# Attention with beacon keys and a maxout feed-forward layer: batch 0 loaded as FP32 by the hardware queue, and a new order of the first two batches

## Chip, cores and metric

One core of one Trainium2 chip (trn2). The metric is the device time of one execution in microseconds (us), the median of several runs; lower is better.

A core has TensorE (PE, with PEld for its weight loads), VectorE (DVE), ScalarE (ACT), GpSimd (POOL) and SyncE (SP), each with its own queue of instructions taken in order. Transfers are asked for by SP, ACT or POOL and carried out by 16 DMA engines. A transfer asked for by POOL (software queue) can change FP32 to BF16 on its way; one asked for by SP or ACT (hardware queue) can't.

## The reference

```python
B, H, S, Nb, D = 8, 8, 576, 16, 64
k_all = concatenate([beacon_k, k], axis=2)            # 592 keys
v_all = concatenate([beacon_v, v], axis=2)
scores = q @ k_all^T / sqrt(D)
scores = where(causal, -1e9, scores)                  # beacons are seen by every query
a = exp(scores - max); a /= a.sum(-1) + 1e-9
x = (a @ v_all).transpose(0, 2, 1, 3).reshape(4608, 512)
h = maximum(maximum(x @ w1, x @ w2), x @ w3)          # 512 -> 768
out = h @ w_out                                       # 768 -> 512, FP32
```

## The kernel before, in words

**Units.** Heads are taken in pairs (32 pairs, `p`), two pairs are a quad (16 quads), two quads a batch. For a pair, queries and keys stand transposed in `qT` and `kT` (128 rows: two heads of 64). `emit_scores` makes scores with keys along the partitions, in four groups for each pair (`groups`), and ACT takes their exponential into `at` (L532). `emit_masks` zeroes what lies above the diagonal, on POOL or on DVE (L549, L551). `emit_pv` multiplies by values and by ones (the sums) for a quad and a half of the tokens (288), four heads side by side in 32 columns of the array each (L592); `invert_sums` and `multiply` (L624) divide into `xT`.

**Feed-forward.** Blocks of 512 tokens; a block has 22 units. For block 0 these are nine `mm1_halves` for the first 256 tokens (kind 0), nine for the others (kind 1), and four `mm2_unit` with `w_out` (kind 2). Other blocks have 18 `mm1_unit` (L654) and four `mm2_unit` (L690). A kind 0 unit needs the first half of batch 0 in `xT`, kind 1 the second half too. `hT` collects the maximum over the three weight matrices on DVE.

**Order.** Each engine's order is the order in which the program is written. Batches 0 and 1, with units laid between them, are written out in `first_steps`; from quad 4 on (batch 2) a loop in `emit_all` follows a table of units, `gaps`, and what is left of the feed-forward ends the kernel. The change touches `first_steps` and what it calls, not the loop.

**Batch 0's queries and keys.** A half (288 tokens) of a pair is 96 rows of 2 heads x 3 tokens x 64. The first halves of pairs 0 and 1 come as FP32 by hardware queues (`load_half`) and are cast by ACT or DVE (`cast_half`, L220); the other three half quads come as BF16 by POOL's software queue (`load_quad`, L229). `turn_half` (L431) transposes with the identity: the two heads do not lie side by side, so each 96x128 transpose is two of 64 columns (L443), to two column places of the array. Batch 1 comes whole by the software queue (`load_whole_quad`), later pairs by SP with a cast on POOL.

**Fillers.** `spare` (L481) multiplies a tile of ones into a bank that is about to be overwritten; `fill` (L411) transposes it. `("scores", p, gi, n)` puts n spares ahead of the scores, `("half", p, h, bank, engine, n, m)` n fills ahead of the keys' transposes and m ahead of the queries'.

**Third key tile of batch 0.** For the first half of the tokens only 48 rows of tile 2 are needed, and `rows_of` (L99) takes just these in L592 and in the masks; the keys behind them are set to zero (L151).

**Gates.** A load with "dve" or "pool" as its last argument has that engine write one element of the destination first, and so waits for that engine's queue.

## Time and profile before

| | us |
|---|---|
| median of 3 runs | 293.68 (293.66 to 293.98) |
| the profiled execution's own time | 294.65 |
| its span, first to last instruction | 292.6 |

| stretch (us) | PE busy | DVE | ACT | POOL | GB/s |
|---|---|---|---|---|---|
| 30 to 40 | 9.91 of 10 | 7.19 | 5.95 | 2.80 | 212 |
| 40 to 50 | 9.32 | 6.85 | 6.38 | 4.52 | 158 |
| 50 to 60 | 9.58 | 7.85 | 8.88 | 5.98 | 222 |
| 60 to 70 | 8.66 | 4.95 | 3.25 | 2.70 | 223 |
| 200 to 250 | 49.52 of 50 | 30.29 | 23.41 | 14.77 | 80 |
| 250 to 292.6 | 39.02 of 42.6 | 20.20 | 5.49 | 0.00 | 50 |

PE's busy time holds fillers, which do no work that is used. GB/s counts bytes as written: a software transfer with cast reads twice as much. The steps of `first_steps` fill PE's first 58 us or so. Over the whole span PE is busy 96%, DVE 58%, ACT 51%, POOL 40%.

### The profile page before, as it was taken

What the parts mean: (1) busy time and instruction counts of PE and PEld (TensorE: products, weight loads), DVE (VectorE), ACT (ScalarE), POOL (GpSimd) and SP (SyncE); (2) the same over time, 40 slices, a digit from 0 to 9 for tenths busy, and PEclk for the clock granted to TensorE, in tenths of its full rate; (3) what the DMA queues carried; (4) which work ended last, traced back from release to release, by engine and by line L of the source; (5) the groups of instructions that cost most, each with busy time, mean ns of one, the idle gap of its engine ahead of it and who ended that gap; (6) DMA issues with size and microseconds to landing.
All of it is one profiled execution on the core that took longest, in us unless ns stands there. A gap on an engine that the chain in (4) does not pass through costs nothing.

```text
span 292.6 us, 8864 instructions
## 1 busy us (share of the span) xinstructions
PE 281.3 (96%) x3714; PEld 160.1 (55%) x3739; DVE 169.6 (58%) x319; ACT 150.5 (51%) x242; POOL 115.8 (40%) x238
## 2 busy tenths in 40 slices
PE   8889999989999999999999999999999999999995
PEld 4656677754454555454545887545454545444442
DVE  1555567837756575566655656565656564474273
ACT  3786576853566676846676256635663552200300
POOL 3618415742546583426454655466323420000000
PEclk9999999999999999999999999999999999999999
DMA  7999979999989999998999899999442003001103
GB/s 131 161 175 185 217 123 225 228 192 261 229 230 256 232 281 270 186 175 263 314 190 181 233 256 268 177 205 214 104 68 98 2 0 137 11 0 74 71 1 143
DMA packets 85111, 49.50 MB, mean 169 GB/s; under 512 B 64208, under 2 KB 79824, under 8 KB 85072
## 3 DMA queue, kind: packets, MB, share of 16 engines
q1 hardware_dynamic: 78864, 43.40, 66.6%
q0 software_dynamic: 5648, 5.21, 11.7%
q8 instruction: 29, 0.48, 0.7%
q10 hardware_dynamic: 560, 0.33, 0.4%
q14 instruction: 10, 0.08, 0.1%
HBM read 35.13 MB, written 14.22 MB: 169 GB/s over the span
## 4 chain that ended last, share of the span: by engine, by line
PE 86%; DMA 7%; POOL 2%; ACT 2%; DVE 1%; issue 1%; POOLq 0%
PE pv L654 21%; PE sc L654 15%; PE wide L654 8%; PE pv L690 6%; PE sc L690 6%; PE sc L517 5%; PE pv L592 4%; DMA w_out_sb<-in_moe_w_out_dram 4%; PE wide L690 3%; PE wide L592 3%; PE sc L592 3%; PE wide L517 3%; DMA w_sb<-in_moe_w_dram 3%; PE pv L481 2%; PE pv L673 1%
## 5 line engine op out<-in xcount | busy, mean ns | idle before, releaser
L532 ACT ACTIVATE at_sb<-sc 128x736 bf16<-128x736 f32 (+5 forms) x91 | 76.5, 867 | 59.3 <-PE sc L517 59.1
L551 POOL TENSOR_SCALAR_AFFINE_SELECT at_sb<-at_sb 128x256 bf16<-128x256 bf16 (+3 forms) x140 | 51.9, 387 | 117.3 <-ACT at_sb L532 117.1
L654 PEld LDWEIGHTS <-w_sb 128*128 128x128 bf16 x648 | 61.1, 98 | 60.4 <-issue 4.7
L654 PE MATMUL pv<-xT,w_sb 128*128 128x512 bf16 (+1 forms) x315 | 65.3, 347 | 0.3
L654 PE MATMUL sc<-xT,w_sb 128*128 128x512 bf16 (+1 forms) x205 | 45.6, 363 | 0.7 <-issue 0.2
L532 ACT ACTIVATE at_sb<-wide 128x736 bf16<-128x736 f32 (+3 forms) x37 | 31.3, 846 | 22.4 <-PE wide L517 22.4
L664 DVE TENSOR_TENSOR hT<-hT,pv 128x512 bf16<-128x512 bf16 x48 | 32.4, 686 | 13.0 <-PE pv L654 13.0
L690 PEld LDWEIGHTS <-hT 128*128 128x128 bf16 x210 | 19.6, 98 | 24.3 <-issue 1.1
L248 POOL CAST p<-st 96x768 bf16<-96x768 f32 x40 | 32.0, 824 | 0.0
L624 DVE TENSOR_TENSOR xT<-pv,recip 128x288 bf16<-128x288 f32 (+2 forms) x48 | 14.2, 350 | 26.7 <-ACT recip L614 26.7
L517 PE MATMUL sc<-qT,kT 64*128 64x288 bf16 (+6 forms) x290 | 27.2, 275 | 2.0 <-POOL at_sb L551 0.6
L664 DVE TENSOR_TENSOR hT<-hT,sc 128x1024 bf16<-128x1024 bf16 (+1 forms) x18 | 19.6, 1098 | 12.7 <-PE sc L654 12.5
L517 PEld LDWEIGHTS <-kT 64*128 64x128 bf16 x400 | 14.9, 94 | 21.8 <-issue 14.7
L592 PEld LDWEIGHTS <-v_sb 128*32 128x32 bf16 (+1 forms) x1408 | 24.7, 96 | 2.6 <-issue 1.3
L654 PE MATMUL wide<-xT,w_sb 128*128 128x512 bf16 (+1 forms) x110 | 24.5, 364 | 0.1
L690 PE MATMUL sc<-w_out_sb,hT 128*128 128x512 bf16 x79 | 19.1, 380 | 1.0 <-DMA w_out_sb<-in_moe_w_out_dram 0.7
L690 PE MATMUL pv<-w_out_sb,hT 128*128 128x512 bf16 x83 | 19.9, 380 | 0.1
L304 POOL CAST v_sb<-st 128x1536 bf16<-128x1536 f32 (+2 forms) x21 | 18.4, 895 | 0.0
L662 DVE CAST hT<-pv 128x512 bf16<-128x512 f32 x20 | 13.7, 688 | 4.8 <-PE pv L654 4.8
L673 PEld LDWEIGHTS <-w_sb 128*128 128x128 bf16 x144 | 13.1, 98 | 3.9 <-issue 1.4
L614 ACT ACTIVATE recip<-lnd 128x288 f32<-128x288 f32 x32 | 14.2, 444 | 1.0
L592 PEld LDWEIGHTS <-ones 128*32 128x32 bf16 (+2 forms) x512 | 11.0, 95 | 6.7 <-issue 4.7
(116 smaller groups left out, 286.3 us busy)
## 6 DMA issues: line engine op xcount, KB each, us to landing
st<-in_q_dram SPq DMA_DIRECT2D x24, 288.0 KB, 5.3
st<-in_k_dram SPq DMA_DIRECT2D x24, 288.0 KB, 5.7
st<-in_v_dram SPq DMA_DIRECT2D x24, 256.0 KB, 5.8
out_dram<-y SPq DMA_DIRECT2D x9, 512.0 KB, 3.3
out_dram<-y SPq DMA_DIRECT2D x17, 256.0 KB, 2.7
w_sb<-in_moe_w_dram POOLq DMA_DIRECT2D x6, 384.0 KB, 7.2
q_dram<-p SPq DMA_DIRECT2D x16, 144.0 KB, 3.1
k_dram<-p SPq DMA_DIRECT2D x16, 144.0 KB, 3.2
```

Of the source, the lines that this page charges most:

```text
L248: cast(t16.rearrange("p r h d -> p h r d"), st[0:QP, i * NQ2 : (i + 1) * NQ2].rearrange("p (h r d) -> p h r d", h=2, r=QR),)
L304: cast(v_sb[0:n, t:t1].rearrange("p t h d -> p (t h d)"), st[0:n, (t - t_lo) * H * D : (t1 - t_lo) * H * D],)
L517: nc.tensor.matmul(ps[:, e, off : off + q1 - q0], kT[hs, 128 * t : 128 * t + 128], qT[hs, q0:q1], start=True, stop=True, tile_position=(64 ...
L532: nc.scalar.activation(out=both_heads(p, gi), in_=ps[:, :, 0 : g_width(p, gi)], func=AF.Exp, scale=scale)
L551: nc.gpsimd.affine_select(out=view, in_=view, compare_op=ALU.is_ge, fill=0.0, base=x0, pattern=[[0, 2], [1, hi - lo]], channel_multiplier=-1,)
L592: nc.tensor.matmul(ps[bank][32 * j : 32 * j + 32, lo + q0 - qa : lo + qb - qa], lhsT, at_view(PPQ * quad + j // 2, t, j % 2, q0, qb), star ...
L614: nc.scalar.activation(out=recip, in_=lnd, func=AF.Exp, scale=-1.0)
L624: nc.vector.tensor_mul(xT[:, 2 * g + part - 1, c0 + ca : c0 + cb], ps[bank][:, lo : lo + cb - ca], recip[:, ca:cb],)
L654: nc.tensor.matmul(dst[:, o0 : o0 + n], w_in[i][:, ct, 128 * (ft + f) : 128 * (ft + f + 1)], xT[:, ct, x0 : x0 + n], start=(ct == 0), stop ...
L664: nc.vector.tensor_max(h, h, ps)
L673: nc.tensor.matmul(ps[:, f], w_in[i][:, ct, 128 * (ft + f) : 128 * (ft + f + 1)], xT[:, ct, tb * TOKB + lo : tb * TOKB + hi], start=(ct == 0),
L690: nc.tensor.matmul(ps[:, t - tt] if two else ps, hT[:, ft, 128 * t : 128 * (t + 1)], w_out_sb[:, ft, :], start=(ft == 0), stop=(ft == n_ft ...
```

## The change

Batch 0's queries and keys all come as FP32 by hardware queues: `load_half` for the first halves of pairs 0 and 1, and the new `load_half_quad` (two pairs in one transfer, into the stage tiles) for the rest. Each half of a pair is cast by an engine named in the step (16 casts for four), and the cast lays the two heads side by side, so that `turn_column` transposes 128 columns at once; batch 1's transposes stay in two. Fills become full transposes there, and spares have 512 columns, not 320. `rows_of` goes: all of the tile's 128 rows are used. The beacons' tiles have 128 rows, the rest zero, and are turned by a plain matmul with the identity. For block 0 the third weight matrix is taken in six units of 512 tokens (kind 3) in place of three units each of kinds 0 and 1, which now have six each. Values may have three banks ("ring+", `passes_3`), without the cut of the last part at `CUT`. `first_steps` is a new list, with other engines for many copies, casts and masks, other fillers and other gates.

```diff
-    K2 = Nb + HALF - 256
-
-    def rows_of(p, t, q1):
-        return K2 if p < PPB and t == 2 and q1 <= HALF else k_rows[t]
...
-    half_pool = ctx.enter_context(tc.tile_pool(name="half", bufs=2))
+    half_pool = ctx.enter_context(tc.tile_pool(name="half", bufs=3))
...
-    bk16_0 = const.tile([Nb, H, D], BF16, name="bk16_0")
+    bk16_0 = const.tile([128, H, D], BF16, name="bk16_0")
+    nc.vector.memset(bk16_0, 0.0)
     bk32_1 = const.tile([NB_PE - Nb, H, D], FP32, name="bk32_1")
-    bk16_1 = const.tile([NB_PE - Nb, H, D], BF16, name="bk16_1")
+    bk16_1 = const.tile([128, H, D], BF16, name="bk16_1")
+    nc.vector.memset(bk16_1, 0.0)
     bk32 = const.tile([NB_DMA, H, D], FP32, name="bk32")
...
-    busy = const.tile([128, 320], BF16, name="busy")
+    busy = const.tile([128, 512], BF16, name="busy")
...
+        stage["half", p, 0, i] = st
+
+    def load_half_quad(g, h, i, queue):
+        key = ("half quad", g, h)
+        st = stage[key] if key in stage else new_stage(key)
+        if i == 1:
+            stage.pop(key)
+        st = st[0:QP, i * NQ2 : i * NQ2 + 4 * HR * D].rearrange("p (h r d) -> p h r d", h=4, r=HR)
+        queue.dma_start(
+            out=st.rearrange("p h r d -> p h (r d)"), in_=half_source(g, h, i, 0, 4)
         )
-        stage["half16", p, 0, i] = t16
+        for j in range(PPQ):
+            stage["half", PPQ * g + j, h, i] = st[:, 2 * j : 2 * j + 2]
+
+    def cast_half(p, i, cast, h=0):
+        t16 = half_pool.tile([QP, HR, 2, D], BF16, name=f"h16{i}")
+        cast(t16.rearrange("p r h d -> p h r d"), stage.pop(("half", p, h, i)))
+        stage["half16", p, h, i] = t16
...
-        ps = sc_psum.tile([128, PPB, n], BF16, name="sc")
+        ps = sc_psum.tile([128, PPB, n], FP32, name="sc")
         for pi in range(PPB):
-            nc.tensor.transpose(
+            nc.tensor.matmul(
                 ps[:, pi],
                 src[:, 2 * pi : 2 * pi + 2].rearrange("p h d -> p (h d)"),
-                ident[0:n, 0:n],
+                ident[:, 0:n],
+                start=True,
+                stop=True,
             )
...
+    def turn_column(dst, src, n):
+
+        if len(src.shape) == 2 and src.shape[1] == 128:
+            nc.tensor.transpose(dst, src, ident[0:n, 0:n])
+            return
+        for e in range(2):
+            nc.tensor.transpose(
+                dst[64 * e : 64 * e + 64],
+                src[:, e],
+                ident[0:n, 0:n],
+                tile_position=(0, 64 * e),
+            )
+
+    def fill(ps, n, wide):
+        src = busy[0:QP, 0:128]
         for i in range(n):
             x0 = 512 + QP * (i % 5)
-            for e in range(2):
-                nc.tensor.transpose(
-                    ps[64 * e : 64 * e + 64, x0 : x0 + QP],
-                    busy[0:QP, 0:64],
-                    ident[0:QP, 0:QP],
-                    tile_position=(0, 64 * e),
-                )
+            turn_column(
+                ps[:, x0 : x0 + QP], src if wide else src.rearrange("p (e d) -> p e d", e=2), QP
+            )
...
-            fill(bank, idle if i == 1 else idle_q)
+            wide = src.shape[1] == HR
+            fill(bank, idle if i == 1 else idle_q, wide)
             for r in range(HR):
-                for e in range(2):
-                    nc.tensor.transpose(
-                        ps[64 * e : 64 * e + 64, r * QP : (r + 1) * QP],
-                        src[:, e, r],
-                        ident[0:QP, 0:QP],
-                        tile_position=(0, 64 * e),
-                    )
+                x = src[:, r].rearrange("p h d -> p (h d)") if wide else src[:, :, r]
+                turn_column(ps[:, r * QP : (r + 1) * QP], x, QP)
             x0 = i * Nb + HALF * h
...
-    def spare(ps, n, cols=320):
+    def spare(ps, n, cols=512):
...
-                    return at[p][0 : rows_of(p, t, q1), off + q0 - lo : off + q1 - lo]
+                    return at[p][0 : k_rows[t], off + q0 - lo : off + q1 - lo]
...
+    passes_2 = [(0, 0, 0, 0, HALF), (1, 1, 0, 0, HALF), (2, 0, HALF, 0, CUT), (2, 1, HALF, CUT, HALF)]
+    passes_3 = [(0, 0, 0, 0, HALF), (1, 1, 0, 0, HALF), (2, 2, 0, 0, HALF)]
...
-                n = rows_of(PPQ * quad, t, qb)
+                n = k_rows[t]
...
+        whole_from = 0 if tb else 2
         if tb == 0:
             for n, lo in ((0, 0), (need, MID)):
-                for i in range(3):
+                for i in range(whole_from):
                     for ft in range(0, n_ft, 2):
                         units.append((n, mm1_halves, (tb, ft, i, lo, lo + MID)))
-        for i in range(0 if tb else 3, 3):
+        for i in range(whole_from, 3):
             for ft in range(n_ft):
...
+    def values(quad, hf, bank="pv"):
+        if bank[:4] == "ring":
+            x = next_tile()
+            banks = [x[:, 0], x[:, 1]]
+        elif bank == "ffn":
+            banks = [ffn_bank() for _ in range(2)]
+        else:
+            banks = [pv_bank(i, [128, 512], FP32) for i in range(2)]
+        if bank == "pv+":
+            banks.append(ffn_bank())
+        elif bank == "ring+":
+            banks.append(single())
+        emit_pv(quad, hf, banks)
...
-        kinds = [2 if f is mm2_unit else int(a[3] == MID) for _, f, a in units[:UPB]]
+        kinds = [
+            2 if f is mm2_unit else 3 if f is mm1_unit else int(a[3] == MID) for _, f, a in units[:UPB]
+        ]
```

The list before, its start:

```python
("load half", 0, 0, "sp"), ("busy", 17), ("identity",), ("busy", 8), ("triangle",), ("load quad half", 1, 0),
("load half", 1, 0, "act"), ("load half", 0, 1, "act"), ("cast half", 0, 1, "dve"), ("load keys 0", "act"),
("cast keys 0", "act"), ("load half", 1, 1, "sp"), ("cast half", 0, 0, "act"), ("cast half", 1, 0, "act"),
("load v0", 0, "dve"), ("half", 0, 0, "ffn", "act", 0, 7), ("cast half", 1, 1, "act"), ("turn keys 0",),
("load v0", 1, "pool"), ("keys", 3, "act"), ("load v0", 2), ("keys", 1, "act"), ("keys", 2, "pool"),
("load quad half", 0, 1), ("half", 1, 0, "ffn", "act", 2, 9), ("scores", 0, 0, 0), ("scores", 1, 0, 3),
("load w", 0), ("cast v0", 0, "pool"), ("half", 3, 0, "ffn", "act", 0, 0), ("mask", 0, 0, "dve"),
("cast v0", 1, "dve"), ("half", 2, 0, "pv", "dve", 4, 0), ("cast v0", 2, "act"), ("scores", 3, 0, 3),
("mask", 1, 0, "pool"), ("scores", 2, 0, 6), ("values", 0, 0, "pv", 0, 4, 0),
("half", 0, 1, "ffn", "act", 0, 7), ("invert",), ("load v0", 3, "dve"), ("scores", 0, 2, 4),
("mask", 3, 0, "dve"), ("mask", 2, 0, "dve"), ("scores", 0, 3, 0), ("multiply",),
("values", 1, 0, "ffn", 0, 4, 0),
...
```

The new list, its start and its end:

```python
("load half", 1, 0, "sp"), ("load half", 0, 0, "sp"), ("identity",), ("cast half", 1, 0, "pool"), ("busy", 12),
("load half", 0, 1, "sp"), ("load keys 0", "act"), ("load v0", 0, "dve"), ("load half", 1, 1, "sp"),
("cast keys 0", "pool"), ("load half quad", 1, 0, 1, "sp"), ("load half quad", 1, 0, 0, "act"),
("turn keys 0",), ("cast half", 0, 0, "act"), ("cast half", 2, 0, "act", 0), ("load half quad", 0, 1, 1, "sp"),
("cast half", 1, 1, "act"), ("cast half", 0, 1, "dve"), ("load half quad", 0, 1, 0, "sp"),
("load v0", 1, "dve"), ("cast half", 3, 1, "act", 0), ("half", 0, 0, "ffn", "dve", 1, 3),
("cast half", 3, 0, "dve", 0), ("scores", 0, 0, 3), ("keys", 3, "act"), ("cast half", 2, 1, "pool", 0),
("half", 2, 0, "ffn", "dve", 4, 4), ("cast v0", 0, "pool"), ("load v0", 2, "dve"), ("keys", 1, "pool"),
("half", 1, 0, "pv", "dve", 1, 2), ("keys", 2, "act"), ("scores", 2, 0, 2), ("triangle",), ("scores", 1, 0, 2),
("load w", 0), ("cast half", 0, 1, "dve", 1), ("half", 3, 0, "ffn", "dve", 4, 3), ("mask", 0, 0, "pool"),
("cast v0", 1, "pool"), ("load v0", 3, "pool"), ("mask", 1, 0, "pool"), ("cast half", 0, 0, "dve", 1),
("scores", 3, 0, 3), ("load half quad", 1, 1, 1, "sp"), ("cast half", 1, 1, "dve", 1),
("cast half", 1, 0, "pool", 1), ("cast v0", 2, "dve"), ("half", 0, 1, "ffn", "act", 0, 7), ("load keys 1",),
("values", 0, 0, "ffn"), ("load half quad", 1, 1, 0, "sp"), ("invert",), ("scores", 0, 2, 3),
("mask", 2, 0, "dve"), ("mask", 3, 0, "dve"), ("multiply",), ("scores", 0, 1, 0), ("values", 1, 0, "ffn"),
("busy", 1), ("invert",), ("half", 1, 1, "pv", "act", 0, 4), ("cast v0", 3, "pool"), ("scores", 0, 3, 0),
("multiply",), ("cast half", 2, 1, "dve", 1), ("cast half", 3, 1, "dve", 1), ("scores", 1, 2, 0), ("busy", 1),
("ffn", "pv", 0), ("scores", 1, 3, 0), ("cast keys 1", "dve"), ("cast half", 3, 0, "dve", 1), ("load v0", 4),
("mask", 1, 3, "dve"), ("mask", 0, 2, "dve"), ("scores", 1, 1, 0), ("ffn", "ffn", 0), ("mask", 0, 3, "dve"),
("load w", 1), ("cast half", 2, 0, "pool", 1), ("cast v0", 4, "act"), ("mask", 0, 1, "dve"),
("ffn", "ring", 0), ("half", 3, 1, "ffn", "act", 0, 2), ("mask", 1, 1, "pool"),
("half", 2, 1, "pv", "dve", 0, 0), ("load quad", 1, 0),
...
("mask", 5, 2, "dve"), ("scores", 5, 3, 0), ("mask", 5, 3, "dve"), ("load", 2, "pool"), ("mask", 4, 2, "dve"),
("load w_out", "pool"), ("scores", 6, 0, 0), ("ffn", "pv", 3), ("scores", 6, 1, 2),
("cast pair", 9, "pool", "pool"), ("values", 2, 0, "ring"), ("keys", 8, "act"), ("invert",), ("multiply",),
("ffn", "pv", 3), ("load", 1), ("mask", 6, 1, "dve"), ("keys", 9, "dve"), ("mask", 6, 0, "pool"),
("scores", 7, 1, 0), ("scores", 6, 2, 0), ("scores", 7, 0, 1), ("scores", 7, 2, 0), ("whole", 8, "pv", "dve"),
("scores", 6, 3, 0), ("cast v", 1, 1), ("values", 2, 1, "ring+"), ("mask", 6, 2, "pool"),
("mask", 6, 3, "pool"), ("invert",), ("mask", 7, 0, "dve"), ("multiply",), ("mask", 7, 2, "dve"),
("scores", 7, 3, 0), ("load", 1, "dve"), ("whole", 9, "ring", "act"), ("ffn", "ring", 3), ("ffn", "pv", 3),
("mask", 7, 3, "dve"), ("mask", 7, 1, "dve"),
```

## Prediction

> **What bounds the kernel now.** I read the page's slices first, then a table by stage, then TensorE's timeline, then the chain of waits. The table's columns are: stretch (us), its length, then busy us of PE, PEld, DVE, ACT, POOL, the granted clock, the DMA share, GB/s.
>
> ```profile
> PE   8889999989999999999999999999999999999995
> ...
> DMA  7999979999989999998999899999442003001103
> ```
> ```profile
> 0.00:10.00 10.00, 8.43 (x96) 5.25 (x97) 2.07 (x18) 4.33 (x12) 3.01 (x13) 1.00 0.85 157
> 10.00:20.00 10.00, 8.78 (x200) 5.54 (x200) 5.37 (x19) 7.67 (x13) 5.48 (x10) 1.00 1.04 145
> 20.00:30.00 10.00, 8.78 (x164) 6.00 (x161) 5.40 (x14) 7.07 (x13) 6.58 (x13) 1.00 1.07 188
> ...
> 150.00:200.00 50.00, 49.79 (x750) 32.39 (x756) 28.73 (x48) 26.75 (x41) 28.02 (x54) 1.00 1.10 224
> ```
>
> From 70 us on TensorE is busy 99.6% (49.79 of 50): it alone sets the time there, and the change doesn't touch that stage. Before it, TensorE idles, though it is fed fillers. So the question is only when the ramp ends. I take as its end the first matmul of L690 (first use of `w_out`), here at 63.18 us. By both orders of instructions that point has the same work behind it (18 of the first block's 22 units, values of quads 0 to 3) and the same list before it (504+144 matmuls of L654's line, 210 of L690's, 1,440 of L592's). What moves that point moves the end by as much.
>
> ```profile
> 1.33 6.33 PE L481 MATMUL pv<-busy 128*128 128x320 bf16 x25 [1.33 <-DVE busy L139]
> ...
> 12.60 0.99 PE L481 MATMUL sc<-busy 128*128 128x320 bf16 x6
> 14.20 0.40 PE L517 MATMUL sc<-qT,kT 64*128 64x288 bf16 x6 [0.61 <-POOL at_sb L551]
> ...
> 18.09 0.59 PE L592 MATMUL fps<-at_sb,ones 128*32 128x288 bf16 x12 [0.44 <-DVE at_sb L549]
> ...
> 29.98 0.83 PE L673 MATMUL fps<-xT,w_sb 128*128 128x256 bf16 x6 [0.59 <-DMA w_sb<-in_moe_w_dram]
> ```
> ```profile
> 63.18 2.76 PE L690 MATMUL sc<-w_out_sb,hT 128*128 128x512 bf16 x11 [0.73 <-DMA w_out_sb<-in_moe_w_out_dram]
> ```
>
> Columns: start, length, and in brackets the idle time before and who ended it. The bracketed waits between 1.4 and 63.2 us (0.18, 0.17, 0.61, 0.44, 0.36, 0.26, 0.59, 0.56, 0.30, 0.56, 0.73) add up to 4.8 us. The 25 matmuls before the first data run at 253 ns, later ones of the same shape at 136 ns ((0.99-0.17)/6, 0.17 being the drain): the array's clock is at half until about 6.4 us, though the granted clock's column says 1.00.
>
> **The change, part by part**, as differences at that point.
>
> *Start.* Two memsets of 256 words stand ahead of the one that starts TensorE, and that one has 512 columns, not 320 (row: 0.33 us for 320). About 0.27 each and 0.20 more: TensorE starts at 2.05, **+0.7**. The 25 cold fillers become 12 of 512 columns: at 267 ns for 320 cold columns (19 of them in 1.33 to 6.4) 427 ns each, 5.1 for 6.3 us: **-1.2**. That stretch then ends near 7.2, not 7.66.
>
> *Warm fillers.* L481's others: 26 x 136 ns = 3.5 us before; after, 31 of 512 columns, 218 ns by the same rate, 6.75: **+3.2**. Fillers ahead of transposes: 29 pairs of half transposes become 35 full ones. Twelve half ones take 0.42 to 0.45 us (L443) and twelve full ones 0.68 (L401); less the drain, 42 ns for a pair and 42 for a full one. So **+0.3**, and the 96 half transposes of batch 0 that become 48 full ones gain nothing of themselves.
>
> *Array shape.* The chain shows the same 44 matmuls (same columns) in the ramp and later:
>
> ```profile
> 14.60 1.34 PE pv L592 x44
> ...
> 80.14 0.79 PE pv L592 x44
> ```
>
> The starts, one by one, show where 0.55 us goes: the four matmuls on 48 rows (`rows_of`) start 96 ns late, and the next on 128 rows 104 ns late. The same 95 to 100 ns stand wherever the tile of the array changes: 28 times of 28 between L654 (128x128) and L517 (64x128). 80 and 96 rows beside 128 cost nothing (L401 beside L654: 2 ns). Taking out `rows_of`, padding the beacons to 128 rows and full transposes (96x128 beside 128x128 fillers) leaves 52 such changes ahead of the point for 69: 17 x 98 ns = **-1.7**. The "ring+" values have one pass for two, with the same 1,152 columns: 0. So have the units of third weights, run whole: 96 x 256 + 24 x 512 for 144 x 256.
>
> *Loads.* Six software transfers of 295 KB (FP32) become hardware ones. Software with cast: 151 GB/s as BF16 in 12 to 14 us, so 302 read. Hardware, same 768-byte lines: 272 GB/s in 2 to 4 us. 1.77 MB take 6.5 us for 5.9: the bytes cost **0.6 us of DMA time**, hidden as long as TensorE has fillers. POOL is rid of six issues (0.70 each, 4.2 us). Twelve casts are added: seven on DVE (0.36, 2.5 us), one on ACT (0.51), four on POOL (96x768 takes 0.82; half, with its fixed part, 0.45). DVE was busy 12.8 of the first 30 us, ACT 19.1: room in the mean, not at each spot. Second halves of quad 0 now land near 10 us, not 15. On ACT's queue one quad transfer waits for the first transfer to land (near 3.3 us): ACT has nothing to do until 7.3, so 0. Pairs 8 and 9 are asked for some 2 us sooner, when DMA idled (0.03 of 42 to 44 us): 0, no wait here rests on them.
>
> *Waits that come in*, each from what stands in line:
> (i) ACT copies the turned beacons (0.17, 0.22) and only then casts pair 0's queries (0.51), though they landed near 4 us; behind stand three more casts. From 7.2: 0.17 drain + 0.1 + 0.2 + 0.5, less 0.13 of fillers: 0.8.
> (ii) both copies of pair 0 on DVE (0.46, 0.37 apart) against 0.65 of fillers: 0.3.
> (iii) the third tile of values: its DMA is gated by a DVE memset behind pair 2's copies, so issued near 11 us; SP's ring before it holds 1.77 MB at 272 GB/s and 0.56 MB of 256-byte lines at 205 (8 to 10 us), done near 11.2. Alone it lands near 14.3, and DVE casts it (0.41). But `moe_w1`'s two transfers start at the same moment (issued by POOL near 10.5, first bytes 2 us later, as at 9.87 to 11.9 here) and take 4.2 us. Shared evenly it lands at 15.4; behind them at 17.9. TensorE is there near 14.9. I take even: wait 0.9, bounds 0 and 3.5. Behind that cast on DVE wait pair 0's second keys and the masks of pairs 2 and 3.
> (iv) the next values for those masks (six, 0.31 each), partly filled: 0.6.
> (v) the first L690 for the max of a double unit (1.22 us on DVE), partly covered: 0.9.
> (vi) the first scores of pair 6 or 7 for DVE's copies: 0.8, as here at 48.00 (0.56). Others 0.5.
> That is 4.8 for 4.8 that go: **0**. `w_out`, asked for near 50 us and 12.4 us under way, is behind two units of 512 columns now, so its 0.73 goes; so do the 0.59 for `moe_w2`, which POOL asks for some 1 us sooner.
>
> Sum: 0.7 - 1.2 + 3.2 + 0.3 - 1.7 + 0 = **+1.3**; fillers that fall into a wait I have also counted take some of it back, so I forecast +1.1. The profiled execution spans 292.6 and took 294.65, the median is 293.68: as difference, 294.8 on the median's scale (293.7 as span).
>
> The Trainium skill, "TensorE: Matmul & The Clock Gate" (Part 1), says the array runs at half clock until about 3.4 us of sustained work have filled a free-running window. The row above agrees with half clock to 6.4 us. By that rule a stretch of 5.1 us, followed by a wait, can miss the window that one of 6.3 us held, and the clock stays low one window longer, not 5.1 us: the third rival below, at about 296.3 for its 297.4.
>
> **Rivals.**
> 1. *Faster: the loads come early enough and the new order has work for each wait.* Second halves lie ready 5 us sooner, so (iii), (iv) and the waits at 18 to 21 and 48 us vanish. Waits left: (i), (ii), (v), 2.0 for 4.8. 1.3 - 2.8 = -1.5: 292.2. It decides from where the third tile lands by 14.5. For: quad loads of the first half land as early as here; DVE, ACT idle half. Against: DVE masks of 0.31 took 0.47 here at 11.6 to 13 beside POOL's casts.
> 2. *The third tile goes behind `moe_w1`'s transfers.* Here values issued at 17.26 moved 29 KB in 18 to 20 us while software moved 325. Wait 3.5 for 0.9: +1.1 + 2.6 = 297.4.
> 3. *Cold clock.* Here the rate rose 5.1 us after the first matmul; the new stretch is 5.1 us long, and wait (i) follows. If the count starts again behind it, all between 7.2 and 13.1 us doubles: some 46 transposes and fillers x 42 ns, 7 x 218 and three scores of 0.2, 4.1 us, of which 1.5 falls into waits (i), (ii) and smaller ones: +2.6, so 297.4. For: the stretch has nothing to spare. Against: any earlier rise saves it.
> 4. *No change: `w_out` lands at 63 as here and both wait for it,* hiding what comes before: 293.7. For: 12.4 us of transfer, gated by POOL. Against: two units stand before it.
>
> **How the numbers follow.** Forecast 0.47, its own range 293.3 to 296.0; rivals 0.25, 0.11, 0.07, 0.10. The range 291.8 to 297.5 takes in most of the first rival, half of the second and third, and leaves less than 2 in 10 out. 0.2% (0.59 us) is about what a measurement here tells from no change. Faster: rival 1 with 0.25, and 0.05 from the forecast's low end: 0.30. Same: rival 4 and 0.05 of the forecast: 0.15. Slower: the rest, 0.55.
>
> **What would show it.** First L481 near 2.05 and first L690-type matmul near 64.3 (rival 1: 61.7; rival 2: 66.9). Array changes: the 44 matmuls of the first values in 0.8 us, not 1.34. Waits: ahead of the first values, 0.9 by DVE's cast. If 320-column and 512-column fillers still run cold past 7.5 us, rival 3. The prediction is wrong if the point moves by less than 0.5 or the stage after 70 us changes its 99.6%.

## The result and the profile after

The changed kernel takes 298.29 us in the median of 4 runs (297.80 to 298.70), the kernel before 293.67 beside it: a ratio of 1.0155, 95% interval 1.0137 to 1.0173, 4.6 us slower. The profiled execution took 298.5 and spans 296.8 (before: 294.65 and 292.6), so the two traces differ by 4.2. The forecast was 294.8, with a range up to 297.5: right in sign, and too small by three quarters.

The 40 slices of TensorE and DMA, then the same table by stage as before, for the changed kernel (stretch, length, busy us of PE, PEld, DVE, ACT, POOL, granted clock, DMA share, GB/s):

```profile
PE   6888999899999999989999999999999999999995
...
DMA  7999999999999989999997899996503002101203
```
```profile
0.00:10.00 10.00, 6.98 (x39) 2.90 (x39) 3.06 (x22) 2.25 (x5) 1.77 (x8) 1.00 0.80 187
10.00:20.00 10.00, 8.40 (x173) 5.12 (x174) 6.81 (x22) 7.99 (x15) 6.49 (x16) 1.00 1.03 201
20.00:30.00 10.00, 8.15 (x110) 5.37 (x111) 6.76 (x19) 5.76 (x11) 3.91 (x7) 1.00 1.10 174
...
100.00:150.00 50.00, 49.19 (x620) 24.96 (x618) 30.67 (x52) 29.11 (x47) 23.64 (x46) 1.00 1.02 235
```

TensorE is busy 1.45 us less in the first 10 us, 0.4 and 0.6 less in the next two stretches. But the fourth row matters too: 49.19 of 50 where the kernel before has 49.69, in the loop that the prediction took as untouched. TensorE's timeline shows which waits these are (start, length, and in brackets the idle time before and who ended it):

```profile
2.08 4.96 PE L495 MATMUL pv<-busy 128*128 128x512 bf16 x12 [2.08 <-DVE busy L136]
7.91 0.30 PE L418 MATMUL fps<-ident,h 96*128 96x96 bf16 x3 [0.64 <-ACT h L229]
10.29 0.30 PE L418 MATMUL fps<-ident,h 96*128 96x96 bf16 x3 [0.48 <-ACT h L229]
...
16.37 0.40 PE L604 MATMUL fps<-at_sb,ones 128*32 128x288 bf16 x12 [0.55 <-DVE kT L465]
16.61 0.62 PE L604 MATMUL fps<-at_sb,v_sb 128*32 128x288 bf16 x32
...
26.76 0.29 PE L418 MATMUL fps<-ident,h 96*128 96x96 bf16 x3 [1.11 <-DVE hT L690]
...
50.89 0.43 PE L604 MATMUL wide<-at_sb,ones 128*32 128x288 bf16 x10 [0.42 <-POOL at_sb L565]
53.69 0.39 PE L495 MATMUL wide<-busy 128*128 128x512 bf16 x1 [0.49 <-DVE xT L633]
...
66.85 3.19 PE L699 MATMUL pv<-w_out_sb,hT 128*128 128x512 bf16 x14 [0.70 <-DVE hT L673]
...
130.21 3.19 PE L699 MATMUL pv<-w_out_sb,hT 128*128 128x512 bf16 x14 [0.81 <-DVE hT L673]
```

With three at 12.23, 18.87 and 21.08 (0.36, 0.41, 0.38), one at 25.35 (0.36) and two at 55.66 and 57.02 (0.20, 0.18) the bracketed waits from the start of TensorE to the 0.70 inside the first product with `w_out` come to 6.3 us, for 4.8 before. To see where the delay arises, I set the starts of each group's values (L592, now L604) side by side, with the feed-forward units issued before each, counted in the two orders of instructions. A quad whose two halves stand together counts as one group.

| values | before, us (units) | after, us (units) | difference | at equal work |
|---|---|---|---|---|
| first | 14.53 (0) | 16.37 (0) | +1.84 | +1.84 |
| third | 27.06 (3) | 29.04 (3) | +1.98 | +1.98 |
| fifth | 49.65 (15) | 50.17 (13) | +0.52 | +2.25 |
| eighth | 80.07 (32) | 81.15 (30) | +1.08 | +2.81 |
| eleventh | 122.88 (62) | 124.34 (60) | +1.46 | +3.19 |
| twelfth | 139.31 (74) | 143.48 (74) | +4.18 | +4.18 |
| end of the span | 292.63 | 296.80 | +4.17 | +4.17 |

From 35 us on the changed kernel has issued two units less at each group of values, 0.866 us each (4 x 216 ns), until it gives them back between 124 and 143 us; the last column adds them. So 2.8 us are lost up to the eighth values, where +1.1 was forecast for the ramp, and 1.4 more in the loop, where nothing was.

### The profile page after: what moved, and what is told of

It is laid out like the page before. It is cut to its first block, busy times and chain, and to the rows that moved or that the text cites. A ratio compares the mean times of both kernels' runs of the same rounds, so it can differ in the third digit from the quotient of the medians.

```text
span 296.8 us, 8668 instructions
## 1 busy us (share of the span) xinstructions
PE 283.6 (96%) x3620; PEld 155.8 (53%) x3620; DVE 175.7 (59%) x329; ACT 149.6 (50%) x238; POOL 114.8 (39%) x239
## 3 DMA queue, kind: packets, MB, share of 16 engines
q1 hardware_dynamic: 81312, 45.17, 66.4%
## 4 chain that ended last, share of the span: by engine, by line
PE 78%; DMA 8%; DVE 5%; ACT 3%; POOL 3%; issue 2%; SPq 1%; POOLq 0%; DVEq 0%; ACTq 0%
PE pv L663 20%; PE sc L663 15%; PE wide L663 8%; PE pv L699 8%; PE sc L699 6%; PE sc L531 5%; PE sc L604 5%; PE pv L604 4%; DMA st<-in_v_dram 3%; PE wide L531 2%; DMA bk<-in_beacon_k_dram 2%; DMA st<-in_q_dram 2%; PE wide L699 1%; ACT at_sb L546 1%; PE wide L604 1%
## 5 line engine op out<-in xcount | busy, mean ns | idle before, releaser
L546 ACT ACTIVATE at_sb<-sc 128x736 bf16<-128x736 f32 (+5 forms) x89 | 74.1, 861 | 54.2 <-PE sc L531 53.8
L663 PEld LDWEIGHTS <-w_sb 128*128 128x128 bf16 x672 | 63.1, 98 | 62.5 <-issue 4.9
L663 PE MATMUL sc<-xT,w_sb 128*128 128x512 bf16 (+1 forms) x232 | 49.8, 364 | 0.0
L546 ACT ACTIVATE at_sb<-wide 128x928 bf16<-128x928 f32 (+3 forms) x39 | 33.6, 862 | 27.4 <-PE wide L531 27.4
L663 PE MATMUL wide<-xT,w_sb 128*128 128x512 bf16 (+1 forms) x124 | 27.7, 366 | 0.0
L699 PE MATMUL pv<-w_out_sb,hT 128*128 128x512 bf16 x108 | 25.7, 380 | 1.5 <-DVE hT L673 1.5
L604 PEld LDWEIGHTS <-v_sb 128*32 128x32 bf16 x1392 | 24.4, 96 | 1.3 <-issue 0.3
L711 DVE COPY y<-pv 128x512 f32<-128x512 f32 x18 | 12.5, 692 | 12.8 <-PE pv L699 12.5
L673 DVE TENSOR_TENSOR hT<-hT,wide 128x1024 bf16<-128x1024 bf16 (+1 forms) x12 | 13.0, 1082 | 10.7 <-PE wide L663 10.6
L604 PEld LDWEIGHTS <-ones 128*32 128x32 bf16 (+1 forms) x512 | 11.1, 95 | 7.5 <-issue 4.8
```

Of the source, the lines that this page charges most:

```text
L546: nc.scalar.activation(out=both_heads(p, gi), in_=ps[:, :, 0 : g_width(p, gi)], func=AF.Exp, scale=scale)
L604: nc.tensor.matmul(ps[bank][32 * j : 32 * j + 32, lo + q0 - qa : lo + qb - qa], lhsT, at_view(PPQ * quad + j // 2, t, j % 2, q0, qb), star ...
L663: nc.tensor.matmul(dst[:, o0 : o0 + n], w_in[i][:, ct, 128 * (ft + f) : 128 * (ft + f + 1)], xT[:, ct, x0 : x0 + n], start=(ct == 0), stop ...
L673: nc.vector.tensor_max(h, h, ps)
L699: nc.tensor.matmul(ps[:, t - tt] if two else ps, hT[:, ft, 128 * t : 128 * (t + 1)], w_out_sb[:, ft, :], start=(ft == 0), stop=(ft == n_ft ...
L711: nc.vector.tensor_copy(y[:, 0:n], ps if two else ps[:, None])
```

## The experiments

18 kernels ran, in six groups, each timed beside the kernel before on the same chip (its medians there: 293.91, 293.95, 294.04, 294.22, 294.36, 293.56). Ratios are to these, with 95% intervals; "above" is the ratio less one, times 293.67.

| run | kernel | median, us | ratio | above, us |
|---|---|---|---|---|
|  | changed kernel | 298.29 | 1.0155 [1.0137, 1.0173] | 4.6 |
| 1 | two more units | 297.32 | 1.0116 [1.0071, 1.0160] | 3.4 |
| 2 | v earlier | 298.81 | 1.0170 [1.0129, 1.0211] | 5.0 |
| 3 | half quad earlier | 297.89 | 1.0152 [1.0101, 1.0204] | 4.5 |
| 4 | before, no 48-row tiles | 293.91 | 0.9998 [0.9969, 1.0026] | -0.1 |
| 5 | units and half quad | 296.47 | 1.0092 [1.0062, 1.0122] | 2.7 |
| 6 | narrow spares | 298.92 | 1.0168 [1.0144, 1.0192] | 4.9 |
| 7 | ScalarE's order | 298.92 | 1.0169 [1.0145, 1.0194] | 5.0 |
| 8 | units, half quad, ScalarE's order | 297.34 | 1.0126 [1.0095, 1.0157] | 3.7 |
| 9 | transfers in order of need | 296.08 | 1.0064 [1.0040, 1.0087] | 1.9 |
| 10 | mask before casts | 296.58 | 1.0090 [1.0063, 1.0116] | 2.6 |
| 11 | both of these | 296.65 | 1.0068 [1.0040, 1.0095] | 2.0 |
| 12 | before, two units less | 303.21 | 1.0304 [1.0274, 1.0335] | 8.9 |
| 13 | third v tile early | 295.98 | 1.0060 [1.0026, 1.0093] | 1.8 |
| 14 | and an earlier start | 297.14 | 1.0106 [1.0079, 1.0132] | 3.1 |
| 15 | values first | 295.57 | 1.0029 [1.0004, 1.0055] | 0.9 |
| 16 | casts by ScalarE | 296.37 | 1.0072 [1.0040, 1.0104] | 2.1 |
| 17 | casts behind the sums | 295.97 | 1.0072 [1.0048, 1.0097] | 2.1 |
| 18 | and v early | 296.64 | 1.0087 [1.0057, 1.0117] | 2.6 |

Most single edits overlap in their intervals with the kernel that they start from; what the times establish is the chain changed kernel, then units and half quad, then values first: 1.0155, 1.0092, 1.0029, with intervals that don't touch. The reverse, two units less in the kernel before, is also clear of noise. No version beat the kernel before. A trace is of one execution, and two traces of the same program can be a microsecond apart, as will be seen; so a trace alone shows a mechanism, not its price.

### The phase of the loop

```diff
         ("ffn", "ring", 3),
         ("ffn", "pv", 3),
+        ("ffn", "pv", 3),
+        ("ffn", "pv", 3),
         ("mask", 7, 3, "dve"),
```

> The changed kernel with two more units of the batch-3 feed-forward at the end of the opening order (18 of them done when the loop starts, as before the change). Phase theory: about 1.4 us of the loss is made in the loop, because the two-unit shift lets the turn from the first to the second product fall inside a run of units (0.70 at 66.85, 0.81 at 130.2). The shift is gone, so 297.0 (1.0 to 1.4 below 298.3), and the first stretch of the loop starts about 1.7 later with equal work behind it. Rival, the loss is all made in the opening and the late delays only carry it: 298.3, no change. Third: the units only move TensorE's work earlier, where it waits for batch 1's values: 298.7 or more.

Measured 297.32, by the ratios 1.2 below the changed kernel. The intervals touch, but in the trace the delay is 2.76 at the eighth values, 2.70 at the twelfth and 2.69 at the last matmul: behind the eighth values this kernel loses nothing. That its opening loses the same 2.8 as the changed kernel's at equal work is partly chance: at the third values, where the two programs are still the same, this execution is already 0.9 us behind the other (29.95 for 29.04). Here is the turn to the second product in it, to be laid beside the 66.85 above:

```profile
63.87 0.63 PE L604 MATMUL pv<-at_sb,v_sb 128*32 128x288 bf16 x32
64.32 0.68 PE L604 MATMUL sc<-at_sb,ones 128*32 128x288 bf16 x20
64.81 1.19 PE L604 MATMUL sc<-at_sb,v_sb 128*32 128x288 bf16 x56
65.94 2.76 PE L699 MATMUL sc<-w_out_sb,hT 128*128 128x512 bf16 x11
```

The values stand between the last unit and the product, 2.3 us in which VectorE takes that unit's maximum. In the changed kernel a double unit stands there instead:

```profile
63.39 1.90 PE L663 MATMUL sc<-xT,w_sb 128*128 128x512 bf16 x8
65.13 1.03 PE L699 MATMUL pv<-w_out_sb,hT 128*128 128x512 bf16 x4
```

Its maximum (1.21 us on VectorE, from 65.58) ends at 66.79, and TensorE stands until 66.85. The loop places its units by what is done when it starts, which is 16 units in the changed kernel and 18 in the kernel before; two fewer moved this turn into a run of units in the first two blocks (66.85 and 130.21).

The reverse, two units taken from the opening of the kernel before (two `("ffn", "pv", 1)` out):

> The kernel before with two feed-forward units fewer in the opening (they are done in the loop instead), so that its loop has the changed kernel's phase. Phase theory: the loop loses 1.2 to 2.7 by VectorE's maximum at the turn between the products, so 295.1 to 296.6, with a step of delay between 123 and 142 us. Rival, the loop's loss comes from something else in the changed kernel's loop (buffers, transfers): 293.9, no change; a gain would say that the opening of the kernel before is limited by those units.

303.21: far more than either theory says, so this is no clean reversal. In the order of its instructions the loop doesn't give the units back but falls further behind, and 7 of them are left behind the last values. Its trace also shows TensorE standing 3.39 us ahead of 98.70 and 1.28 ahead of 61.21, for which the profile names no releaser. How much of the 8.9 us each part makes was not separated. What it does show is the same wait, in a kernel that had none of its kind, at two turns (timeline of that kernel, L690 and L654 being lines of the kernel before):

```profile
65.37 1.46 PE L690 MATMUL pv<-w_out_sb,hT 128*128 128x512 bf16 x6 [0.63 <-DVE hT L683]
...
130.27 1.02 PE L654 MATMUL pv<-xT,w_sb 128*128 128x512 bf16 x4 [0.54 <-DVE hT L664]
```

### The second half of batch 1's keys

(The edit's label says quad 1 of batch 0: `first_steps` numbers the pairs of batch 0 in two quads, and this is the second half of its second quad's keys. The expectations call it batch 1's keys, which is a slip of words; the step is the one shown.)

```diff
         ("load v0", 1, "dve"),
+        ("load half quad", 1, 1, 1, "sp"),
...
-        ("load half quad", 1, 1, 1, "sp"),
         ("cast half", 1, 1, "dve", 1),
```

> The changed kernel with the second half of batch 1's keys asked for by SyncE right behind the first v, about 10 us sooner. Theory: its late landing (23.39, behind moe_w1's transfers) holds VectorE 1.63 us at its cast, the copies of the hidden units behind it are late and TensorE stops 0.36 and 1.11 at 25.35 and 26.76; with the keys there in time those go: 296.8 to 297.3 (1.0 to 1.5 below). Rival, the earlier transfer takes the place of the third v tile and TensorE stops there instead: 298.0 to 299.4. Third: the stall only moves to the next late landing: 298.3.

By the median alone nothing (1.0152). By its trace the waits of 0.36 and 1.11 are gone, the third values start at 27.62 for 29.04, and the end comes 1.3 sooner. The step from the eighth values to the end is still in it: 2.7 us from 0.16 to 2.87, of which 1.7 are the two units given back and 1.0 is lost. VectorE in the changed kernel, then in this one:

```profile
23.39 0.62 DVE L229 CAST h<-st 96x384 bf16<-96x384 f32 x2 [1.63 <-DMA st<-in_k_dram]
23.93 0.68 DVE L690 CAST hT<-pv 128x512 bf16<-128x512 f32 x1
```
```profile
22.13 0.68 DVE L229 CAST h<-st 96x384 bf16<-96x384 f32 x2
23.10 0.69 DVE L690 CAST hT<-pv 128x512 bf16<-128x512 f32 x1 [0.29 <-PE pv L682]
```

There the cast waits for a transfer and TensorE's hidden units wait behind the cast; here VectorE waits for TensorE. Both edits together:

> The changed kernel with both the two more units at the end of the opening (first experiment) and the earlier request for the second half of batch 1's keys (third). The two losses are held to be separate: one made at 20 to 30 us, the other in the loop. Then the gains add: 1.2 plus 0.9 to 1.3, so 296.0 to 296.4, and behind the first loop block the delay against the kernel before stays constant, with none of the 2.7 us step between 123 and 142 us that the third experiment's trace shows. Rival, both repair one and the same thing (units late against VectorE's maximum): 297.2, no better than the better one of them.

296.47: the first theory at its upper edge. In its trace the delay is 1.4 at the eighth values and 1.5 at the end, so the loop's step is gone, and the ratio's interval no longer touches the changed kernel's.

### Fillers and array shapes

```diff
-        spare(ps[:, 0], idle)
+        spare(ps[:, 0], idle, 320)
```

> The changed kernel with the spare matmuls ahead of the scores 320 columns wide instead of 512 (31 of them, 218 to 136 ns each, 2.5 us of TensorE's time less). If the wide fillers lie on the path, as the prediction put it (+3.2): the first values start 1.0 to 1.5 us earlier and the time falls by 2 to 2.5, to 296. Rival, TensorE waits for what the fillers cover: waits of the same sum appear in their place (ScalarE and VectorE copies named as releasers), no change, 298.3. Third, the clock falls where TensorE now stands idle: slower than 298.7.

2.5 us of TensorE's work taken out, and the median doesn't fall: 298.92. The profiled execution gains 0.6. So as a whole the fillers were not a cost of 2.5. Part of what they took was time in which TensorE would have waited: between the fourth and the eighth values, where ten of them stand and 0.8 us came out, the stretch is no shorter in the trace (45.92 us for 45.65), and the wait at 50 us grew from 0.42 to 1.05. The first values, with ten more fillers ahead of them and again 0.8 less, came 0.39 sooner. In the kernel before, with `rows_of` returning the full count of rows:

> The kernel before with the 48-row tiles of the first pairs given the full row count, as the changed kernel has it, and nothing else. Theory: each change of the array's row shape costs about 0.1 us, ten of them go: 292.7 (1.0 below 293.67). Rival, the shape changes lie in time in which TensorE would wait anyway: 293.7. Where the rows added cost a longer copy: 293.9.

293.91, the same time to within 0.3%. The theory was 1.0; its profiled span is 0.75 shorter, but the profiled execution before was itself 1.0 above its median, so nothing is left of it that the times show. This tests only `rows_of`, ten of the 17 changes of array shape that the prediction counts, or 1.0 of its 1.7 us; the padded beacons and the full transposes were not tested.

### ScalarE's first work

```diff
-        ("turn keys 0",),
         ("cast half", 0, 0, "act"),
-        ("cast half", 2, 0, "act", 0),
+        ("turn keys 0",),
...
-        ("cast half", 3, 1, "act", 0),
...
+        ("cast half", 2, 0, "dve", 0),
         ("cast half", 3, 0, "dve", 0),
         ("scores", 0, 0, 3),
+        ("cast half", 3, 1, "act", 0),
```

> The changed kernel with another order of ScalarE's first work: the cast of pair 0's queries ahead of the beacons' copies, the cast of pair 2's queries on VectorE, that of pair 3's keys behind the first exponential. Theory: ScalarE stands 1.86 us for the landing of the quad's queries with three casts ahead of the first exponential, and this gives the waits of 0.64 at 7.91, 0.48 at 10.29 and 0.36 at 12.23; those shrink, the first exponential starts 1.4 sooner, and the time falls by 0.5 to 1.0 (297.3 to 297.8). Rival, the first values' start is set by VectorE's copies into the bank behind (the 0.55 at 16.37), which stay where they are: first values at 16.4 again and 298.3.

298.92, no gain by the times (the intervals overlap), and 1.0 slower in the trace: a miss, and the most useful one. ScalarE's first exponential starts 1.75 sooner (9.21), and TensorE is through its first scores and the fills behind them 0.7 sooner, only to find that the next transfer hasn't landed (1.80 for a cast of VectorE that waits for the quad's queries, then 0.62 for GpSimd's). Then this happens (table by stage of this kernel; the clock is the third column from the right):

```profile
9.00:10.00 1.00, 0.07 (x2) 0.00 (x0) 0.00 (x0) 1.00 (x2) 0.00 (x0) 1.00 1.14 240
10.00:11.00 1.00, 0.13 (x3) 0.13 (x4) 0.54 (x2) 0.23 (x1) 0.00 (x0) 1.00 1.16 229
11.00:12.00 1.00, 0.38 (x8) 0.24 (x7) 0.54 (x2) 0.72 (x3) 0.60 (x2) 1.00 1.20 183
12.00:14.00 2.00, 2.00 (x22) 0.92 (x22) 1.62 (x5) 0.56 (x1) 1.93 (x6) 0.84 0.48 86
14.00:16.00 2.00, 2.00 (x21) 1.45 (x21) 0.64 (x2) 1.49 (x2) 1.90 (x6) 0.50 1.05 219
```

TensorE works 0.58 of the 3 us to 12, and for some 3 us behind that its clock is half. DMA is full all those 3 us. So an earlier start of ScalarE alone gains nothing here, as the next transfers land no sooner; and in this execution TensorE pays twice, for the stand and for the clock behind it. The same edit on the units and half quad:

> All three edits together: two more units, the earlier half of keys, ScalarE's new first order. If the three losses are separate, 295.0 to 295.9, still 1.3 to 2.2 slower than the kernel before, so about a third of the loss would lie elsewhere (wide fillers, copies behind VectorE's masks). If the third edit does nothing: 296.0 to 296.4. Equal to the kernel before (293.7) would say that the loss was nothing but these places in the order.

297.34, 0.9 above the kernel without it. The intervals overlap, so the loss isn't clear of noise, but a gain there is again none.

### The order of the first transfers

First, on the kernel with units and half quad: what is needed first is asked for first.

```diff
-        ("load v0", 0, "dve"),
         ("load half", 1, 1, "sp"),
...
         ("cast half", 0, 0, "act"),
+        ("load half quad", 0, 1, 1, "act"),
+        ("load half quad", 0, 1, 0, "act"),
...
         ("cast half", 0, 1, "dve"),
+        ("load v0", 0, "dve"),
-        ("load half quad", 0, 1, 0, "sp"),
-        ("load v0", 1, "dve"),
-        ("load half quad", 1, 1, 1, "sp"),
...
         ("half", 0, 0, "ffn", "dve", 1, 3),
+        ("load v0", 1, "dve"),
...
         ("scores", 0, 0, 3),
+        ("load half quad", 1, 1, 1, "act"),
```

> The kernel of the fifth experiment (units and earlier half quad, 296.5) with the first transfers in the order in which they are needed: first v behind the queries and keys of all four pairs' first halves, second halves of quad 0 asked for by ScalarE after its first cast (about 7.9 instead of 4.4 and 5.0), the second v tile behind those, the second half of quad 1's keys behind the first scores. Nothing else moves. Theory: the first halves of pairs 2 and 3 land at 9.7 because 0.8 MB that is not needed yet is moved beside them (0.2 MB per us in all); now they land by about 8.5, the wait of 0.5 at 10.3 goes, the first exponential starts 1 us sooner, first values at 15.7 or before (16.7 now), 295.5 to 296.0. Rival, the order of the transfers is worth nothing since the next late landing (second halves, v) stops TensorE as long: 296.5. Slower than 296.8 if a second half of pair 0 now lands behind its cast.

The waits for the quad (0.54 and 0.46 in the kernel it is built on) are gone; the first exponential starts at 9.92. Seven of 13 executions are at 295.1 to 296.1, the others reach up to 302.4. The profiled one, 301.16, is one of the two longest, so it isn't typical of the kernel; its timelines of VectorE and TensorE show what it stood for:

```profile
21.05 0.43 DVE L322 CAST v_sb<-st 128x512 bf16<-128x512 f32 x1 [6.66 <-DMA st<-in_v_dram]
21.39 0.45 DVE L465 COPY kT<-fps 128x288 bf16<-128x288 bf16 x1
```
```profile
21.90 0.62 PE L604 MATMUL fps<-at_sb,ones 128*32 128x288 bf16 x12 [6.92 <-DVE kT L465]
```

The cast is that of the third v tile, asked for at 11.2 and now behind more transfers; the copy behind it frees the bank of the first values. Run 11, whose transfers have the same order, was profiled in an execution of 295.51: there the tile landed 5.2 us after its request, not 9.7, its cast started at 16.07 and TensorE waited 1.57 at the first values. So the next run asks for it at about 9, ahead of `moe_w1`:

```diff
+        ("load v0", 0, "pool"),
+        ("load half quad", 0, 1, 1, "sp"),
+        ("load half quad", 0, 1, 0, "sp"),
...
         ("cast half", 0, 1, "dve"),
+        ("load v0", 1, "dve"),
...
         ("half", 0, 0, "ffn", "dve", 1, 3),
+        ("load v0", 2, "dve"),
```

(Against the changed kernel; the same steps are taken out where they stood. The edit also lets each half quad take one staging tile instead of two.)

> The kernel with the transfers in the order of need, now gated so that the queues are never empty and the third v tile is asked for at about 9 instead of 11.2 us, ahead of moe_w1 and of the second half of quad 1's keys; each half quad takes one staging tile instead of two. Theory: the spread of the ninth experiment (295.1 to 302.4) is the third v tile: asked for behind the keys and beside moe_w1's transfers it lands anywhere from 15 to 21 us, VectorE's cast of it stands ahead of the copy that frees the bank of the first values (6.92 us in the profiled execution), and TensorE's clock falls to half for the 6 us behind it. Sooner asked for, all executions lie at 294.8 to 296 and the granted clock is 1.0. Rival, the stall belongs to another landing (second halves of pair 0): the spread stays, upper runs over 298.

295.98, the same median; the longest of 9 executions is 298.17 (302.4 there). Over all kernels, 6 of 25 executions with the order of need (runs 9 and 11) took 299 us or more, and 1 of 52 with the third tile asked for early (runs 13 to 18). That fits a tile that sometimes lands late, but only one of those long executions was profiled, so it isn't shown for the others. VectorE still waits for the tile:

```profile
14.62 0.58 DVE L320 CAST v_sb<-st 128x512 bf16<-128x512 f32 x1 [1.13 <-DMA st<-in_v_dram]
15.12 0.44 DVE L463 COPY kT<-fps 128x288 bf16<-128x288 bf16 x1
```
```profile
15.62 0.61 PE L602 MATMUL fps<-at_sb,ones 128*32 128x288 bf16 x12 [1.61 <-DVE kT L463]
```

Two edits that only let TensorE and ScalarE start sooner, on top:

> The same with VectorE's fill of the busy tile ahead of its other fills (TensorE can start about 0.5 earlier) and the cast of pair 0's queries ahead of the beacons' copies on ScalarE. Theory: the remaining 1.2 us against the kernel before hold 0.7 of the later start and 0.64 of the wait at 7.9; 293.8 to 294.8, level with the kernel before. Rival, the first halves' landing sets the first scores: as the run before it, 294.8 to 296. Third, TensorE gets through its fillers sooner, stands still longer and the clock falls: over 297 in some executions.

297.14: nothing gained. TensorE starts at 1.54, not 2.09, and waits 2.03 at the first values, not 1.61. What is left is a count of bytes. Between 8 and 16 us the kernel with the third v tile early moves 226 to 229 GB/s in each stretch, without a pause. Ahead of the third v tile it asks for 0.59 MB (second halves of quad 0) that the kernel before asked for at 9.87, behind its v tiles. So, the first values ahead of that half again, as before the change:

```diff
         ("load v0", 1, "dve"),
+        ("load v0", 2, "dve"),
+        ("load half quad", 0, 1, 1, "sp"),
+        ("load half quad", 0, 1, 0, "sp"),
...
-        ("half", 0, 1, "ffn", "act", 0, 7),
...
-        ("values", 0, 0, "ffn"),
+        ("values", 0, 0, "pv"),
+        ("half", 0, 1, "ffn", "act", 0, 7),
```

(The edit also puts the cast of the third v tile ahead of that half's cast.)

> The kernel of the run before last (296.0; transfers in order of need) with the first values ahead of the second half of pair 0, as the kernel before has it: the three v tiles are asked for ahead of quad 0's second halves, their casts stand ahead of those halves' casts, and the turn of that half stands behind the first values (which take the other bank pair). Theory: the queues move 0.225 MB per us without a pause from 2 to 20 us, so what is asked for ahead of the third v tile sets the first values: 0.59 MB less is 2.6 us sooner for the landing, VectorE no longer stands 1.1 at that cast, the first values start at 14 to 14.6 (15.6 there, 14.5 before the change) and the wait of 1.6 ahead of them goes: 294.6 to 295.2 and a clock of 1.0. Rival, the halves that now land later stop TensorE behind the first values instead by as much: 296.0.

The first values start at 13.58 (their main part at 14.25), 2.0 sooner and ahead of the kernel before. 11 of 12 executions are at 296.51 or less, and 10 of 12 have a mean granted clock of 0.998 or more. The time is 295.57, 1.0029 [1.0004, 1.0055]: of the 4.6 us some 0.9 are left. The order of the transfers and that of TensorE's work were changed together here, so how much each gave is not separated.

### What is left: 48 to 60 us

At the fourth values this kernel is 0.41 ahead of the kernel before with the same units done, at the eighth 1.15 behind. Two waits stand between, 1.39 at 50.08 (for a mask of GpSimd) and 0.48 at 52.84. Four runs were aimed at them, two early and two late.

> The changed kernel with batch 1's v asked for by GpSimd right after w instead of behind VectorE's place in the order (36.6 us). Theory: GpSimd stands 5.6 us before its casts of v (46.7 landing), which makes the masks late and stops TensorE 0.42 at 50.89 and 0.49 at 53.69; with v asked for about 4.5 us sooner those go: 297.4 to 297.9 (0.4 to 0.9 below). Rival, those waits are taken by other work or come back at w_out, which is then issued or landed at another time: 298.3. A loss (over 298.6) would say that the earlier transfer delays w_out or the moe weights.

(On the changed kernel; `("load v", 1, 0, "pool")` right behind `("load w", 2)`.) Nothing gained, 298.81. In the trace the values at 50 started 0.5 sooner and then waited 2.84 for VectorE's masks; but the profiled execution, 301.62, is the longest of the six (the others 298.36 to 299.21), so this wait is not typical of them.

> The kernel of the fifth experiment (296.5) with one mask of pair 5 on GpSimd ahead of the two casts of pair 8 (1.8 us) instead of behind them. Theory: TensorE's waits of 0.98 at 50.3 (for that mask) and part of the 0.48 at 53.1 go: 295.4 to 296.0. Rival, the exponential of that mask's scores or VectorE's masks are as late, since VectorE's mask multiplications stand still while GpSimd casts (1.4 and 1.8 us for work of 0.25 us each): the wait is put down to VectorE and 296.5 stays.

(On units and half quad; `("mask", 5, 0, "pool")` ahead of `("cast pair", 8, "pool", "pool")`.) 296.58, no gain, and the rival's reason: the wait is now VectorE's. Its masks and GpSimd's casts in that kernel, then TensorE:

```profile
49.40 1.79 DVE L563 TENSOR_TENSOR at_sb<-at_sb,tri 128x256 bf16<-128x256 bf16 x2 [0.22 <-ACT at_sb L546]
```
```profile
49.40 1.65 POOL L254 CAST p<-st 96x768 bf16<-96x768 f32 x2
```
```profile
51.24 0.28 PE L604 MATMUL wide<-at_sb,ones 128*32 128x176 bf16 x8 [1.03 <-DVE at_sb L563]
```

Both edits of this group:

> Both edits, the transfers in the order of need and the mask ahead of the casts, on the kernel of the fifth experiment. If both theories hold and the losses are separate: 294.4 to 295.5; the kernel before is at 293.9. If only one holds: its own value again. If neither: 296.5.

296.65, its best execution 294.61; the mask's edit adds nothing to the transfers' order. Then GpSimd's two casts were given to ScalarE, on the kernel with the values first:

```diff
-        ("cast pair", 8, "pool", "pool"),
...
         ("scores", 5, 3, 0),
+        ("cast pair", 8, "act", "act"),
...
-        ("load", 2, "pool"),
...
         ("load w_out", "pool"),
+        ("load", 2, "pool"),
```

> That kernel with the two casts of pair 8 (1.8 us) on ScalarE behind the last scores of pair 5 instead of on GpSimd, and w_out asked for ahead of the next pair's transfers. Theory: VectorE's mask multiplications stand still while GpSimd casts (0.9 us for 0.28, ending with the cast), which is the 0.8 to 1.0 wait ahead of the values at 50; without the casts there the masks take 0.25 to 0.3 each and the wait goes: 0.7 to 1.2 below the run beside it. Rival, the mask is late by its exponential alone, and ScalarE's casts delay the next exponentials: no gain, or 0.5 to 1.5 slower.

296.37. The mechanism is as the theory has it, the gain as the rival has it: the two masks take 0.49 us together, not 1.79, and the values at 48.09 don't wait, but the sums' reciprocals now stand behind ScalarE's casts:

```profile
47.58 0.49 DVE L561 TENSOR_TENSOR at_sb<-at_sb,tri 128x256 bf16<-128x256 bf16 x2 [0.16 <-ACT at_sb L544]
```
```profile
52.41 0.39 PE L493 MATMUL wide<-busy 128*128 128x512 bf16 x1 [1.43 <-DVE xT L631]
```

The casts behind the sums instead (`("cast pair", 8, "act", "act")` after the `("invert",)` of those values):

> The kernel with the first values ahead of the second half of pair 0 (295.6), with the casts of pair 8 on ScalarE as in the run before, but behind the logarithm and exponential of the first values of pairs 4 and 5, so that they delay none of these. Theory: in the run before, VectorE's masks took 0.25 us each without GpSimd's casts beside them and the wait of 1.39 at 50 went, but ScalarE's casts (1.56) pushed the sums' reciprocals back and 1.43 came back at 52.4; with the casts behind them both waits go: 294.2 to 294.8. Rival, the casts now delay the exponentials of pairs 6 and 7 and the wait moves on: 295.6 or more.

295.97: the rival. 0.61, 0.48, 0.50 and 0.47 at 49.8 to 55.5, two of them for exponentials.

> The same with batch 1's v asked for by GpSimd right after w (as in the second experiment), about 4 us sooner. Theory: GpSimd no longer stands 6.2 us for its landing, the masks behind it are done in time, and the second experiment gained nothing only because GpSimd's casts then stood beside VectorE's masks (3.0 us for one of 0.25): now 293.6 to 294.5, level with the kernel before (294.2 to 294.4 beside it) or faster. Rival, the masks are not late by that landing: as the run before it. Slower than it by 1 or more if VectorE's masks stand still again.

296.64, and the theory's condition wasn't met: v was asked for 4.8 us sooner (30.54 for 35.39) but landed only 0.5 sooner, and GpSimd still stood 6.55 us for it (6.88 without the edit). The wait at 50 is gone, and 0.61 comes at 45.17 for a whole quad that landed later; 0.52, 0.50 and 0.47 stay. In this stretch most waits that were removed came back on another engine. One thing was not tried on its own: the ten fillers that the change put into it (two in the kernel before):

```profile
L495 PE MATMUL sc<-busy 128*128 128x512 bf16 x9 | 2.5, 381 | 0.0
```

That is the group in the changed kernel between 35.5 and 81.15 us (busy us and mean ns of one, then the idle time before them: none). With one more of the kind they are ten, for two of 320 columns before; from start to next start they take 2.57 us, for 0.47. That is 2.1 us more of TensorE's time than before. Between the fourth and the eighth values the kernel with the values first takes 47.49 us, of which TensorE idles 2.37; the kernel before takes 45.94 and idles 2.58. So in this stretch the waits are no longer than before, and the difference is busy time, which the fillers more than cover. Yet the narrow spares took some of it out on the changed kernel, and a wait grew in its place; what it is worth stays open.

## Why the prediction failed, point by point

- **Start and cold fillers, +0.7 and -1.2:** as forecast. TensorE starts at 2.08 and the 12 fillers end at 7.04 (7.66 before). As run 14 shows, an earlier start by itself gains nothing.
- **Warm fillers, +3.2:** wrong as a term of a sum. 2.5 us of them came out without a gain. A filler costs only where TensorE would not have waited; the sum booked all of them with waits beside them, and took back only 0.2 for those that fall into a wait.
- **Array shape, -1.7:** the rows were as forecast (the 44 matmuls of the first values end 0.86 us after they start, for 1.4 before). As time it doesn't show where it was tested: taking `rows_of` out of the kernel before, 1.0 of the 1.7, gives 0.9998. The other 0.7 no run tests.
- **Loads, "hidden", and "ACT has nothing to do until 7.3, so 0":** the first step that failed. Six software transfers became hardware ones; four are asked for by 5 us, two at 15.7 and 18.7. The quad's queries land at 9.7 with three of ScalarE's casts ahead of its first exponential (10.96 for 9.99); the transfer asked for at 15.7 lands at 23.4 and holds VectorE, and with it TensorE's units. What an early transfer costs is shown by the reordered kernels: with the three v tiles asked for ahead of quad 0's second halves the first values start at 13.58, behind these halves at 15.62.
- **Waits, 4.8 for 4.8:** 6.3. (i) was 0.64 for 0.8, (v) 0.70 for 0.9, behind the first four matmuls of the product: right. (iv) was 0.41 for 0.6: right in size, but the profile names a multiply of VectorE as what ended it, not the masks. (ii) and (vi) didn't come. (iii) was 0.55 for 0.9, but for another reason: the v tile's cast (15.16) waited for nothing, and what TensorE waited for was VectorE's copy of pair 0's second keys, which TensorE itself had turned only just before, at 15.40 to 15.82. (The 205 GB/s in (iii) is a misreading: that row, 8 to 10 us of the kernel before, says 259.) Not foreseen were 0.48 and 0.36 behind ScalarE's casts, 0.36 and 1.11 for the late keys, 0.42 and 0.49 at 50 us: 3.2 us.
- **The point and the stage behind it:** the first second product came at 65.13, 0.8 beyond the 64.3, with the same 18 units before it in both kernels, as the prediction says. But "What moves that point moves the end by as much" failed: the point moved 1.95 us and the end 4.17. And with it failed "the change doesn't touch that stage". TensorE went on only at 66.85, and two of the 18 units are now done inside the loop, which starts with 16. That decides where each turn falls, and from the eighth values to the end it cost 1.4 us.
- **Rivals:** faster (0.25): its condition, the third tile landed by 14.5, was missed by little (it landed near 14.7), but its waits didn't go. The third tile behind `moe_w1`: not in the changed kernel, where its cast waits for nothing, but 6.92 us of stall in one execution of a reordered one. Cold clock: the fillers run at full rate behind 7 us (three of 512 columns in 0.81 at 8.22), so not there; later in the opening it came in the traces of several experiments. `w_out` is waited for no longer, against the fourth rival, and the point came no sooner for it.

In one line: up to the eighth values +2.8 for +1.1 (transfers and the queues of ScalarE and VectorE behind them), the loop behind +1.4 for 0. For the loop the cause is shown by the order of instructions, the traces and the two units; for the opening by the chain of reordered kernels as a whole, while the parts of the 2.8 are read from single traces.
